# Second products of five groups of a fused FNet and SwiGLU block put into Strassen's form

## The chip, the cores and the metric

The kernel runs on one core of a Trainium2 chip. The metric is device time in microseconds of one execution, taken over several runs. The core's engines are named as in the profile: PE (TensorE, matmuls), PEld (its weight loads), DVE (VectorE), ACT (ScalarE), POOL (GpSimd) and SP (SyncE, which here issues loads). Each works off its own queue of instructions in order.

## The reference

One block of a network on 2048 rows of 512 columns, in float32. The condition `c` gives six vectors, shifts, scales and gates. The first half is a Fourier mixing of the modulated layer norm, the second a gated feed-forward with 1792 inner columns:

```python
x = x + ga * _A_ref(h, ...)                   # real part of a DFT over rows and columns
h = _layernorm(x, axis=-1) * (1 + cb) + sb
gate = jnp.einsum("bsd,df->bsf", h, w1)       # "first products"
up   = jnp.einsum("bsd,df->bsf", h, w3)
hh   = _silu(gate) * up
out  = jnp.einsum("bsf,fd->bsd", hh, w2)      # "second products"
x = x + gb * out
```

The change touches only the feed-forward, and in it only the second products.

## The kernel before

**Precision.** A float32 operand is split into a high part (an ACT copy that rounds to fp32r, `copy`, L87) and a low part (a DVE subtraction, `minus`, L90). `product` (L98, its matmul in L100) then makes three passes: high by high, high by low, low by high. The weights are the stationary operand, the activations move.

**Tiles.** Everything is held with columns on the 128 partitions and rows along the free dimension, in row blocks t = 0 to 3 of 512 rows. The inner 1792 columns are seven groups g of 256. Row blocks are worked in two pairs, (0, 2) as pair 0 and (1, 3) as pair 1. An item is a group with a pair. Items 0 to 4 are groups 2 to 6 of pair 0, items 5 to 11 are groups 0 to 6 of pair 1.

**First products of an item.** They are already in the Strassen-Winograd form: seven units a1 to a7 for w1 and b1 to b7 for w3, made by `factor`. A unit is six matmuls into one PSUM bank (two column blocks of 128 by three passes). The units chain: a6, a7 and a4 are added in the bank of a1 after the running sum was read, a3 in that of a5. The left operands are w, and sums of quarters of w (`w1s`, `w3s`), each with its high and low; the right operands are the normalized rows h2 and sums of them (h2h, h2l, th, tl). The units' banks are copied or added out by ACT (x, L87; Silu into v, L1224) and DVE (x and v, L93; v<-v,x, L96). `result` makes the product v of gate and up and then its parts hf, the high on ACT and the low on DVE.

**Second products before.** For each row block t and each block d of 128 output columns there is one unit, `down_unit`: six matmuls (two inner column blocks by three passes) into one bank, banks 6 and 7 in turn. So there are eight units, called y in the order, to an item. ACT copies the bank, scaled by gb, into half of a tile y (L335), and after every second unit POOL issues an accumulating DMA (L1146) of the 512 KB tile y into a buffer `sums` in HBM. Each row block and half of the output columns has such a buffer. The last two groups of pair 1 don't go to HBM: their units are added by DVE (L1137) to a tile xr, which `load_sums` (L1106) fetches from `sums` after group 4.

**What sets the order.** The units are written out by hand, one string to an item (`body`, after a `head` that ends the item before):

```python
body = "a6 a5 y a7 y y a4 y a3 y b1 y b2 y b6 b5 y"          # L1661
head = ... else "-b7 a1 a2 -b4 -b3 " if i else "a1 a2 "       # L1666
```

A minus means a unit of the item before. The y units in a body belong to the item before too, so the second products of items 5 to 9 stand in the bodies of items 6 to 10. Below, "the first to the fifth body" are these, each counted from its first unit, -b7, to the next body's. Item 5, where the pair changes, is `turning`.

Preparing a weight is five steps (`weight_jobs`, L1164): the high (ACT), four sums of quarters (DVE, 128x256 each), the low (DVE), the high of the sums (ACT), the low of the sums (DVE). w2 had two (`plain_jobs`): high and low. Steps wait in a list `jobs`. After each unit `beside` lets as many of them out as a credit of DVE and ACT time allows (`advance`), and where a unit needs a weight that isn't ready, `drain` lets everything ahead of it out at once. w1 of the next item is put in the list at a3, w2 of the same item at b2, w3 of the next item at b3. `behind(n, fn)` issues an operation n units later.

## Time and profile before

The time is 708.48 us, the median of 3 runs (707.67 to 708.64). The profiled execution took 708.46 us; its span, from the first to the last instruction, is 706.7 us, so 1.8 us lie around it.

| stretch, us | what runs | PE busy | DVE busy | ACT busy | DMA share |
|---|---|---|---|---|---|
| 60 to 276 | DFT over rows | 214.18 of 216.00 | 191.66 | 123.39 | 0.63 |
| 276 to 477 | feed-forward, mostly pair 0 | 197.15 of 201.00 | 166.60 | 134.40 | 0.56 |
| 477.00 to 501.25 | item 5, where the pair changes | 24.25 of 24.25 | 15.79 | 17.73 | 0.78 |
| 501.25 to 652.63 | the first to the fifth body | 151.17 of 151.38 | 92.34 | 92.36 | 0.59 |
| 652.63 to 706.70 | the last group and the end | 45.91 of 54.07 | 31.18 | 13.71 | 0.29 |

How to read it: a matmul of 512 columns is shown 0.39 us long, but the next starts 0.227 us after it, so busy times of PE overlap and a stall under 0.16 us does not show as idle time. The distance from start to start is the measure. On DVE and ACT, too, the next instruction can start shortly before the shown end of the one ahead. The DMA share is the mean busy share of the 16 DMA engines.

### The profile page before, as it was taken

What the parts mean: (1) busy time and instruction counts of PE and PEld (TensorE: products, weight loads), DVE (VectorE), ACT (ScalarE), POOL (GpSimd) and SP (SyncE); (2) the same over time, 40 slices, a digit from 0 to 9 for tenths busy, and PEclk for the clock granted to TensorE, in tenths of its full rate; (3) what the DMA queues carried; (4) which work ended last, traced back from release to release, by engine and by line L of the source; (5) the groups of instructions that cost most, each with busy time, mean ns of one, the idle gap of its engine ahead of it and who ended that gap; (6) DMA issues with size and microseconds to landing.
All of it is one profiled execution on the core that took longest, in us unless ns stands there. A gap on an engine that the chain in (4) does not pass through costs nothing.

```text
span 706.7 us, 8912 instructions
## 1 busy us (share of the span) xinstructions
PE 686.3 (97%) x3152; PEld 564.7 (80%) x3152; DVE 548.3 (78%) x877; ACT 430.8 (61%) x709; POOL 119.4 (17%) x141
## 2 busy tenths in 40 slices
PE   7999999999999999899999999999999999999995
PEld 4898888888888888687888788787788888888784
DVE  5999679997999978579987886896865556664763
ACT  4998865545454655745677676867665565656420
POOL 1320253542524000200100101011010100101000
PEclk9999999999999999999999999999999999999998
DMA  8730299796678521522868558376763847537403
GB/s 266 211 120 1 77 373 328 251 307 229 207 283 287 168 86 41 92 58 64 209 114 199 89 130 153 61 156 137 239 136 73 180 62 175 111 69 162 137 0 124
DMA packets 38100, 108.93 MB, mean 154 GB/s; under 512 B 4896, under 2 KB 5152, under 8 KB 38048
## 3 DMA queue, kind: packets, MB, share of 16 engines
q0 software_dynamic: 12352, 43.00, 29.3%
q1 hardware_dynamic: 25264, 63.98, 27.5%
q10 hardware_dynamic: 432, 1.31, 0.5%
q8 instruction: 26, 0.43, 0.3%
q14 instruction: 26, 0.21, 0.1%
HBM read 76.81 MB, written 33.55 MB: 156 GB/s over the span
## 4 chain that ended last, share of the span: by engine, by line
PE 81%; DVE 7%; ACT 6%; issue 2%; DMA 2%; SPq 1%; ACTq 0%; DVEq 0%
PE bank L100 52%; PE bank L750 25%; PE bank L559 2%; PE bank L598 1%; DMA wmr<-in_wmr 1%; ACT xc L894 1%; PE bank L576 1%; DVE xc L96 1%; SPq L231 1%; ACT hf L87 1%; ACT y L335 1%; DVE v L96 0%; DVE hl L90 0%; ACT hm L501 0%; DMA w<-in_wdi 0%
## 5 line engine op out<-in xcount | busy, mean ns | idle before, releaser
L100 PE MATMUL bank<-hf,w2h 128*128 128x512 f32 (+1 forms) x452 | 140.9, 391 | 0.3
L1146 POOL DMA_DIRECT2D sum<-y x48 | 41.0, 855 | 390.1 <-ACT y L335 373.0
L100 PEld LDWEIGHTS bank<-hf,w2h 128*128 128x128 f32 x452 | 84.3, 188 | 22.1 <-DVE hf L90 3.4
L100 PE MATMUL bank<-hf,w2l 128*128 128x512 f32 (+1 forms) x226 | 87.6, 388 | 0.0
L87 ACT ACTIVATE hf<-v 128x512 fp32r<-128x512 f32 x56 | 35.3, 630 | 67.3 <-DVE v L96 62.7
L335 ACT ACTIVATE y<-bank,gb 128x512 f32<-128x512 f32 x96 | 64.9, 682 | 18.6 <-PE bank L100 18.3
L93 DVE TENSOR_TENSOR v<-bank,x 128x512 f32<-128x512 f32 x36 | 24.7, 685 | 34.9 <-PE bank L100 34.8
L750 PE MATMUL bank<-bh,us 128*128 128x512 f32 x128 | 49.9, 390 | 0.0
L93 DVE TENSOR_TENSOR x<-bank,x 128x512 f32<-128x512 f32 x36 | 24.7, 687 | 32.4 <-PE bank L100 28.7
L750 PE MATMUL bank<-bh,ul 128*128 128x512 f32 x128 | 49.8, 389 | 0.0
L750 PE MATMUL bank<-d,us 128*128 128x512 f32 x128 | 49.8, 389 | 0.0
L750 PE MATMUL bank<-d,uh 128*128 128x512 f32 x128 | 49.8, 389 | 0.0
L750 PE MATMUL bank<-l,us 128*128 128x512 f32 x128 | 49.8, 389 | 0.0
L750 PE MATMUL bank<-l,uh 128*128 128x512 f32 x128 | 49.8, 389 | 0.0
L100 PEld LDWEIGHTS bank<-hf,w2l 128*128 128x128 f32 x226 | 42.4, 188 | 8.4
L90 DVE TENSOR_TENSOR hf<-v,hf 128x512 fp32r<-128x512 f32 x56 | 38.5, 687 | 12.2 <-ACT hf L87 12.1
L170 POOL DMA_INDIRECT re<-in_ctr,mirror x32 | 35.8, 1117 | 66.2 <-DVE ul L90 39.5
L1224 ACT ACTIVATE v<-v 128x512 f32<-128x512 f32 x36 | 22.8, 632 | 38.8 <-DVE v L93 38.8
L87 ACT ACTIVATE x<-bank 128x512 f32<-128x512 f32 x72 | 41.4, 586 | 7.2 <-PE bank L100 6.5
L170 POOL DMA_INDIRECT im<-in_cti,mirror x32 | 32.7, 1023 | 35.3 <-PE bank L750 10.0
L100 PE MATMUL bank<-h2h,w1h 128*128 128x512 f32 x80 | 31.8, 397 | 1.5 <-ACT h2h L87 1.5
L100 PE MATMUL bank<-h2l,w1h 128*128 128x512 f32 x80 | 31.9, 399 | 0.8 <-DVE h2l L90 0.8
(246 smaller groups left out, 1775.2 us busy)
## 6 DMA issues: line engine op xcount, KB each, us to landing
sum<-y POOLq DMA_DIRECT2D x48, 512.0 KB, 5.6
w<-in_w SPq DMA_DIRECT2D x42, 512.0 KB, 4.5
re<-in_ctr SPq DMA_DIRECT2D x32, 256.0 KB, 5.0
im<-in_cti SPq DMA_DIRECT2D x32, 256.0 KB, 5.0
wmc<-in_wmc SPq DMA_DIRECT2D x8, 512.0 KB, 6.3
xr<-in_xt SPq DMA_DIRECT2D x8, 512.0 KB, 7.6
sum<-xr SPq DMA_DIRECT2D x8, 512.0 KB, 6.2
x<-in_x SPq DMA_DIRECT2D x11, 256.0 KB, 4.8
```

Source lines behind the costliest of these rows:

```text
L87: nc.scalar.activation(dst, src, AF.Copy, scale=scale)
L90: nc.vector.tensor_tensor(out=dst, in0=a, in1=b, op=OP.subtract)
L93: nc.vector.tensor_tensor(out=dst, in0=a, in1=b, op=OP.add)
L96: nc.vector.tensor_tensor(out=dst, in0=a, in1=b, op=OP.mult)
L100: nc.tensor.matmul(acc, lhs[a], rhs[b], start=first and n == 0, stop=last and n == len(PASSES) - 1, skip_group_check=more,)
L170: nc.gpsimd.indirect_dma_start(dst, None, rows, bass.IndirectOffsetOnAxis(ap=at, axis=0))
L231: queue.dma_start(raw_w[dt][q * 64 : (q + 1) * 64, m, :], w[i][par::2, q])
L335: nc.scalar.activation(dst, src, AF.Identity, scale=by)
L559: nc.tensor.matmul(halves(hb[k])[:, m, :], sides((hh, hl)[a][k])[:, dt, m, :], wu[dt][:, b, m, :], start=False, stop=dt % 2 == 1 and n == ...
L750: nc.tensor.matmul(acc[what, e], lhs, rhs, start=begin and i == 0, stop=(end or (turn and what == "x")) and i == len(terms) - 1, skip_grou ...
L1146: nc.gpsimd.dma_start(sums[t, d // 2], y, accum_op=OP.add)
L1224: behind(k != 0 or q == 0, lambda: nc.scalar.activation(v, src, AF.Silu))
```

## The change

The second products of items 5 to 9 (groups 0 to 4 of pair 1, `SEVEN`) take the same form as the first ones: seven units (`seven_unit`) in place of eight, in the order 2, 5, 3, 1, 6, 7, 4. A unit is again six matmuls: two output column blocks e, in banks 6 and 7, by three passes. Units 2, 5 and 1 start the two banks anew. The others are added to what stands there after it was read: 3 to 5, and 6, 7 and 4 to 1. ACT reads both banks after every unit, so there are 14 copies to a group in place of 8 and 7 accumulating DMAs in place of 4.

The right operands are three of the products v as they are and four sums of them, made by DVE in place in the tiles v (`seven_parts`, spread over eight units); each of the seven gets a high and a low, before there were four. The left operands are w2 and sums of its quarters, so w2 takes the five steps of `seven_jobs` in place of two. In the turning item w2 is put in the list at b3 in place of b2. In items 6 to 9 w3 of the next item is put there at b6, at the end of the body, in place of b3. The bodies with seven y have the order `"a6 a5 a7 y a4 y a3 y b1 y b2 y b6 y b5 y"`. `load_sums` for both row blocks comes after the last unit.

```diff
--- before.py
+++ after.py
@@ -1208,6 +1208,12 @@
     TO = {1: 0, 6: 0, 7: 0, 4: 0, 2: 1, 5: 2, 3: 2}
     state, vs = {}, {}
 
+    SEVEN = [(g, 1) for g in range(NG - 2)]
+    ORDER7 = (2, 5, 3, 1, 6, 7, 4)
+    LEFT7 = {1: "h0", 2: "h2", 4: "h3", 5: "s0", 6: "s1", 7: "s2", 3: "s3"}
+    TO7 = {2: (0, 0), 5: (1, 1), 3: (0, 1), 1: (0, 0), 6: (0, 1), 7: (1, 1), 4: (1, 0)}
+    right7, banks7 = {}, []
+
     def right(pair, n):
         t0, t1 = PAIRS[pair]
         if n in (1, 2, 3):
@@ -1224,6 +1230,9 @@
             behind(k != 0 or q == 0, lambda: nc.scalar.activation(v, src, AF.Silu))
             return
         times(v, v, src)
+        if (g, pair) in SEVEN:
+            seven_parts(i, q, k)
+            return
 
         def highs():
             hf[g, PAIRS[pair][k], q] = take(F32R, "hf")
@@ -1235,6 +1244,105 @@
 
         behind(1, highs)
         behind(2, lows)
+
+    def seven_parts(i, q, k):
+        key = items[i]
+        v = {(a, b): vs[i][a][:, b, :] for a in range(2) for b in range(2)}
+
+        def high(n, src):
+            right7[key, n] = take(F32R, "hf")
+            copy(right7[key, n][:, 0, :], src)
+
+        def low(n, src):
+            u = right7[key, n]
+            minus(u[:, 1, :], src, u[:, 0, :].bitcast(F32))
+
+        if (q, k) != (0, 1):
+            n = {(0, 0): 1, (1, 0): 2, (1, 1): 3}[q, k]
+            behind(1, lambda: high(n, v[q, k]))
+            behind(2, lambda: low(n, v[q, k]))
+            return
+        t1, t2, t3, t4 = v[0, 0], v[1, 1], v[0, 1], v[1, 0]
+        behind(1, lambda: minus(t1, v[0, 1], v[0, 0]))
+        behind(2, lambda: high(5, t1))
+        behind(2, lambda: minus(t3, v[1, 1], v[0, 1]))
+        behind(3, lambda: low(5, t1))
+        behind(3, lambda: minus(t2, v[1, 1], t1))
+        behind(4, lambda: high(7, t3))
+        behind(4, lambda: minus(t4, v[1, 0], t2))
+        behind(5, lambda: high(6, t2))
+        behind(5, lambda: low(7, t3))
+        behind(6, lambda: high(4, t4))
+        behind(7, lambda: low(6, t2))
+        behind(8, lambda: low(4, t4))
+
+    def seven_jobs(key):
+        use = wuse[key] = {}
+
+        def highs():
+            use["h"] = take(F32R, "w2h")
+            copy(flat(use["h"]), flat(wraw[key]))
+
+        def totals():
+            use["s"] = take(F32, "w2s")
+            s, r = four(use["s"]), four(wraw[key])
+            plus(s[:, 0, :], r[:, 1, :], r[:, 3, :])
+            minus(s[:, 1, :], s[:, 0, :], r[:, 0, :])
+            minus(s[:, 2, :], r[:, 0, :], r[:, 1, :])
+            minus(s[:, 3, :], r[:, 2, :], s[:, 1, :])
+
+        def lows():
+            use["l"] = take(F32R, "w2l")
+            r = wraw.pop(key)
+            minus(flat(use["l"]), flat(r), flat(use["h"]).bitcast(F32))
+            give(r)
+
+        def sum_highs():
+            use["sh"] = take(F32R, "w2sh")
+            copy(flat(use["sh"]), flat(use["s"]))
+
+        def sum_lows():
+            use["sl"] = take(F32R, "w2sl")
+            minus(flat(use["sl"]), flat(use["s"]), flat(use["sh"]).bitcast(F32))
+            give(use.pop("s"))
+            done.add((key, "l"))
+
+        step(jobs, 1, highs, 0.0, 1.0)
+        step(jobs, 1, totals, 1.4)
+        step(jobs, 1, lows, 1.2)
+        step(jobs, 1, sum_highs, 0.0, 1.0)
+        step(jobs, 1, sum_lows, 1.2)
+
+    def seven_unit(g, pair, n, key):
+        new = n in (1, 2, 5)
+        if new:
+            banks7[:] = [bank(6), bank(7)]
+        y = take(F32, "y")
+        which, k = TO7[n]
+        t = PAIRS[pair][k]
+        names = ("h", "l") if LEFT7[n][0] == "h" else ("sh", "sl")
+        u = right7.pop(((g, pair), n))
+        for e, to in enumerate(banks7):
+            at = int(LEFT7[n][1]) * HALF + e * P
+            product(
+                to,
+                [flat(wuse[key][x])[:, at : at + P] for x in names],
+                [u[:, b, :] for b in range(2)],
+                new,
+                True,
+                not new,
+            )
+            d = 2 * which + e
+            copy_by(y[:, e, :], to, gb[:, d : d + 1])
+        give(u)
+        nc.gpsimd.dma_start(sums[t, which], y, accum_op=OP.add)
+        behind(4, lambda: give(y))
+        if n == ORDER7[-1]:
+            for x in wuse.pop(key).values():
+                give(x)
+            if g == NG - 3:
+                for t in PAIRS[pair]:
+                    load_sums(t)
 
     def factor(i, w, n):
         g, pair = items[i]
@@ -1280,7 +1388,7 @@
             behind(1, lambda: give(st["x"]))
             if w == "w3":
                 for x in vs.pop(i):
-                    behind(3, lambda x=x: give(x))
+                    behind(9 if items[i] in SEVEN else 3, lambda x=x: give(x))
 
 
     loads.extend((n, m) for n in range(len(steps)) for m in range(2))
@@ -1576,10 +1684,14 @@
                 up_block(g, t, q, w)
                 beside(2.72, USED[w])
 
-    def down(g, pair, t, d, key):
+    def down(g, pair, *which):
+        key = which[-1]
         drain(lambda: (key, "l") in done, jobs)
         delayed()
-        down_unit(g, pair, t, d, key)
+        if (g, pair) in SEVEN:
+            seven_unit(g, pair, *which)
+        else:
+            down_unit(g, pair, *which)
         beside(1.36, USED["own" if pair == 1 and g >= NG - 2 else "y"])
 
     for w in ("w1", "w3"):
@@ -1617,6 +1729,9 @@
             for n in PLACE:
                 give(h.pop((0, n)))
         sum_parts(jobs, *sums_of.pop())
+
+    def early_w3(i):
+        return items[i] in SEVEN and i != turning
 
     def unit(kind, i, n):
         g, pair = items[i]
@@ -1638,8 +1753,8 @@
         if (kind, n) == ("a", 3) and more:
             load_w(("w3", *items[i + 1]))
             weight_jobs(i + 1, "w1")
-        if (kind, n) == ("b", 2):
-            plain_jobs(("w2", g, pair))
+        if (kind, n) == ("b", 3 if i == turning else 2):
+            (seven_jobs if (g, pair) in SEVEN else plain_jobs)(("w2", g, pair))
         if (kind, n) == ("b", 3):
             if i + 2 == turning:
                 drain(lambda: ("xc", 3) in done)
@@ -1648,10 +1763,15 @@
                 sums_of.append(pair_sums(background, 1))
             if i + 1 == turning:
                 other_operands()
-            if more:
+            if more and not early_w3(i):
                 weight_jobs(i + 1, "w3")
-            for t in PAIRS[pair]:
-                seconds.extend((g, pair, t, d, ("w2", g, pair)) for d in range(ND))
+            if (g, pair) in SEVEN:
+                seconds.extend((g, pair, n, ("w2", g, pair)) for n in ORDER7)
+            else:
+                for t in PAIRS[pair]:
+                    seconds.extend((g, pair, t, d, ("w2", g, pair)) for d in range(ND))
+        if (kind, n) == ("b", 6) and more and early_w3(i):
+            weight_jobs(i + 1, "w3")
         beside(1.36, FACTOR[kind][n])
 
     weight_jobs(0, "w3")
@@ -1659,6 +1779,8 @@
     ln2(3)
     for i in range(len(items)):
         body = "a6 a5 y a7 y y a4 y a3 y b1 y b2 y b6 b5 y"
+        if i and items[i - 1] in SEVEN:
+            body = "a6 a5 a7 y a4 y a3 y b1 y b2 y b6 y b5 y"
         if i == turning:
             body = "y y y y y a6 y a5 y a7 y b1 b2 a4 b6 a3 b5"
         if i == len(items) - 1:
```

How the queues change is shown at two places. The first is DVE's queue in the first body. The rows stand between the product v of b3 and the addition that reads a7's bank (`v_...<-bank0`); w3s, w3l and w3sl are the sums and the lows of w3 for this body, w2s, w2l and w2sl those of w2, hf the lows of the products. Before:

```order
L93 TENSOR_TENSOR w3s_717_4617<-w3_700_4539 128x256
L90 TENSOR_TENSOR w3s_717_4617<-w3s_717_4617,w3_700_4539 128x256
L90 TENSOR_TENSOR w3s_717_4617<-w3_700_4539 128x256
L90 TENSOR_TENSOR w3s_717_4617<-w3_700_4539,w3s_717_4617 128x256
L90 TENSOR_TENSOR hf_715_4605<-v_661_4328,hf_715_4605 128x512
L90 TENSOR_TENSOR w3l_720_4634<-w3_700_4539,w3h_716_4615 128x1024
L90 TENSOR_TENSOR hf_718_4623<-v_660_4327,hf_718_4623 128x512
L90 TENSOR_TENSOR w3sl_724_4648<-w3s_717_4617,w3sh_721_4636 128x1024
L93 TENSOR_TENSOR v_712_4584<-bank0_709_4575,x_723_4646 128x512
```

The same stretch with the change; `v_660<-v_660`, `v_660<-v_661,v_660` and `v_661<-v_661,v_660` are the first three sums of products:

```order
L93 TENSOR_TENSOR w2s_715_4613<-w2_687_4444 128x256
L90 TENSOR_TENSOR w2s_715_4613<-w2s_715_4613,w2_687_4444 128x256
L90 TENSOR_TENSOR w2s_715_4613<-w2_687_4444 128x256
L90 TENSOR_TENSOR w2s_715_4613<-w2_687_4444,w2s_715_4613 128x256
L90 TENSOR_TENSOR hf_713_4601<-v_661_4328,hf_713_4601 128x512
L90 TENSOR_TENSOR v_660_4327<-v_660_4327 128x512
L90 TENSOR_TENSOR w2l_717_4629<-w2_687_4444,w2h_714_4611 128x1024
L90 TENSOR_TENSOR v_660_4327<-v_661_4328,v_660_4327 128x512
L90 TENSOR_TENSOR w2sl_722_4645<-w2s_715_4613,w2sh_718_4631 128x1024
L90 TENSOR_TENSOR hf_719_4633<-v_660_4327,hf_719_4633 128x512
L90 TENSOR_TENSOR v_661_4328<-v_661_4328,v_660_4327 128x512
L93 TENSOR_TENSOR v_710_4580<-bank0_707_4571,x_721_4643 128x512
```

Where w3's preparation stood, w2's stands with three sums and a low between its steps, and the addition from a7's bank follows all of it; w3's preparation comes behind.

The second place is ACT's queue at the end of the second to fourth body, from the high of b2's product (hf) on. x are copies of the banks of b6 and b5, y copies of the second products' banks. Before, from the second body:

```order
L87 ACTIVATE hf_788_5000<-v_754_4819 128x512
L335 ACTIVATE y_789_5002<-bank6_790_5003,gb_152 128x512
L87 ACTIVATE x_782_4974<-bank3_781_4967 128x512
L87 ACTIVATE x_792_5026<-bank5_791_5019 128x512
L335 ACTIVATE y_789_5002<-bank7_793_5028,gb_152 128x512
```

And with the change, in the second body; y_803, y_808 and y_814 are the tiles of units 6, 7 and 4:

```order
L87 ACTIVATE hf_802_5043<-v_769_4867 128x512
L335 ACTIVATE y_803_5045<-bank6_796_5015,gb_152 128x512
L335 ACTIVATE y_803_5045<-bank7_797_5016,gb_152 128x512
L87 ACTIVATE w2sh_805_5057<-w2s_801_5038 128x1024
L87 ACTIVATE x_794_5011<-bank3_793_5004 128x512
L87 ACTIVATE w3h_807_5069<-w3_787_4979 128x1024
L335 ACTIVATE y_808_5071<-bank6_796_5015,gb_152 128x512
L335 ACTIVATE y_808_5071<-bank7_797_5016,gb_152 128x512
L87 ACTIVATE x_811_5093<-bank5_810_5086 128x512
L87 ACTIVATE w3sh_813_5097<-w3s_809_5081 128x1024
L335 ACTIVATE y_814_5099<-bank6_796_5015,gb_152 128x512
```

Five instructions have become eleven, and two preparing steps stand between the copies of unit 6 and those of unit 7, a third between those of 7 and 4.

## Prediction, on record before the run

> **What bounds the kernel now.** I read the share of the engines first, then the windows of the five bodies, then single rows of the timeline.
>
> ```profile
> span 706.7 us, 8912 instructions
> PE 686.3 (97%) x3152; PEld 564.7 (80%) x3152; DVE 548.3 (78%) x877; ACT 430.8 (61%) x709; POOL 119.4 (17%) x141
> ```
>
> Then the windows of the five bodies, a row each: length, then busy time of PE, PEld, DVE, ACT, POOL, the granted clock, the DMA share and GB/s.
>
> ```profile
> 501.25:531.97 30.72, 30.51 (x134) 24.62 (x132) 20.94 (x32) 19.40 (x29) 2.56 (x3) 1.00 0.63 162
> 531.97:562.13 30.16, 30.16 (x133) 24.70 (x132) 17.85 (x27) 18.25 (x27) 3.40 (x4) 1.00 0.59 122
> 562.13:592.30 30.17, 30.17 (x133) 24.70 (x132) 17.85 (x27) 18.24 (x27) 3.41 (x4) 1.00 0.59 122
> ...
> 622.46:652.63 30.17, 30.17 (x133) 24.70 (x132) 17.85 (x27) 18.23 (x27) 3.41 (x4) 1.00 0.52 99
> ```
>
> PE is never without work there, and DVE and ACT have 12 us free of 30. So PE's own time is what a body costs. How much is that to a unit?
>
> ```profile
> 503.44 0.50 PE L100 MATMUL bank<-h2h,w1l 128*128 128x512 f32 x1 [0.21 <-DVE w1l L90]
> ...
> 508.60 0.39 PE L100 MATMUL bank<-th,w1sh 128*128 128x512 f32 x1
> ...
> 509.96 0.39 PE L100 MATMUL bank<-th,w1sh 128*128 128x512 f32 x1
> ...
> 602.84 0.19 PEld L100 LDWEIGHTS bank<-hf,w2h 128*128 128x128 f32 x1 [0.38 <-DVE hf L90]
> ```
>
> The rows at 508.60 and 509.96 are the first matmuls of a6 and a5: a unit takes 1.36 us, a matmul 0.227. A body of 22 units would be 29.92 us. The 0.25 to 30.17 is one wait for the low of a product (last row); the first body has 0.55 more at a1, which waits for w1's low (first row).
>
> **What the change removes.** Five units, 30 matmuls: 6.80 us, if nothing else waits. A body of 21 units is 28.56 us.
>
> **What it adds.** To each group, on ACT, 6 copies y, 3 highs and one high of w2's sums; on DVE 3 lows, 4 sums of products, 4 sums of quarters and one low. The prices are distances from start to start, where instructions stand back to back:
>
> ```profile
> 508.80 0.69 DVE L93 TENSOR_TENSOR x<-bank,x 128x512 f32<-128x512 f32 x1 [0.67 <-PE bank L100]
> 509.52 0.69 DVE L96 TENSOR_TENSOR v<-v,x 128x512 f32<-128x512 f32 x1
> 510.13 0.42 DVE L93 TENSOR_TENSOR w3s<-w 128x256 f32<-128x256 f32 x1
> 510.59 0.43 DVE L90 TENSOR_TENSOR w3s<-w3s,w 128x256 f32<-128x256 f32 x1
> 510.93 0.42 DVE L90 TENSOR_TENSOR w3s<-w 128x256 f32<-128x256 f32 x1
> 511.27 0.42 DVE L90 TENSOR_TENSOR w3s<-w,w3s 128x256 f32<-128x256 f32 x1
> 511.60 0.68 DVE L90 TENSOR_TENSOR hf<-v,hf 128x512 fp32r<-128x512 f32 x1
> 512.21 1.22 DVE L90 TENSOR_TENSOR w3l<-w,w3h 128x1024 fp32r<-128x1024 f32 x1
> 513.34 0.68 DVE L90 TENSOR_TENSOR hf<-v,hf 128x512 fp32r<-128x512 f32 x1
> 513.94 1.22 DVE L90 TENSOR_TENSOR w3sl<-w3s,w3sh 128x1024 fp32r<-128x1024 f32 x1
> ```
>
> On DVE: 0.61 for 128x512 (0.72 where the next needs its result), 1.47 for four sums of quarters, 1.13 for 128x1024.
>
> ```profile
> 602.28 1.06 ACT L87 ACTIVATE w3sh<-w3s 128x1024 fp32r<-128x1024 f32 x1 [0.41 <-DVE w3s L90]
> 603.24 0.58 ACT L87 ACTIVATE x<-bank 128x512 f32<-128x512 f32 x1
> 603.72 0.68 ACT L335 ACTIVATE y<-bank,gb 128x512 f32<-128x512 f32 x1
> ...
> 610.43 0.69 ACT L335 ACTIVATE y<-bank,gb 128x512 f32<-128x512 f32 x1 [0.76 <-PE bank L100]
> 611.01 1.05 ACT L87 ACTIVATE w1h<-w 128x1024 fp32r<-128x1024 f32 x1
> ...
> 618.81 0.64 ACT L87 ACTIVATE hf<-v 128x512 fp32r<-128x512 f32 x1 [1.30 <-DVE v L96]
> 619.35 0.67 ACT L335 ACTIVATE y<-bank,gb 128x512 f32<-128x512 f32 x1
> ```
>
> On ACT: 0.96 for a high of a weight, 0.48 for x, 0.58 for y, 0.54 for hf. No row shows the sums of products as such; the lows (687 ns mean) and v<-v,x (692) have the same shape, which bounds them within 1%. So a group's ACT work grows by 6 x 0.58 + 3 x 0.54 + 0.96 = 6.1 us and DVE's by 7 x 0.61 + 1.47 + 1.13 = 6.9. On the busy rows that is 24.3 and 24.8 of 28.56 us: enough in sum, but with little left for a bad place. What counts, then, is where work is in front of something that PE waits for. A hand-over costs this:
>
> ```profile
> 323.49 0.57 ACT L87 ACTIVATE x<-bank 128x512 f32<-128x512 f32 x1
> ...
> 324.11 0.19 PEld L100 LDWEIGHTS bank<-th,w1sh 128*128 128x128 f32 x1 [0.65 <-ACT x L87]
> ...
> 324.45 0.40 PE L100 MATMUL bank<-tl,w1sh 128*128 128x512 f32 x1
> ...
> 592.30 0.39 PE L100 MATMUL bank<-th,w3sh 128*128 128x512 f32 x1
> ...
> 592.50 0.69 ACT L335 ACTIVATE y<-bank,gb 128x512 f32<-128x512 f32 x1 [0.76 <-PE bank L100]
> ```
>
> The copy ends at 324.06 and the second matmul after it is at 324.45, so the first began in effect at 324.22: 0.16 us after the end. In the other direction a reader starts 0.20 us after the next unit's first matmul.
>
> **First body, DVE.** Up to v<-v,x at 509.52 nothing has changed. Behind it the order now has four sums of w2, a low, a sum, w2's low, a sum, the low of w2's sums, a low, a sum, and only then the addition that reads a7's bank. From 510.13: +1.47 is 511.60, +0.61 +0.61 is 512.82, where w2's low starts; it ends at 514.04. The first y unit is three units after 508.60 and its third matmul, the first with that low, 0.45 later, at 513.13; it starts at 514.20, 1.07 late. DVE goes on: 512.82 + 1.13 + 0.60 + 1.14 + 0.61 + 0.61 = 516.91 for the addition, which ends at 517.60. Unit a4 is added in the bank that it reads, so a4 starts at 517.76, where the order alone would give 508.60 + 4 x 1.36 = 514.04: **3.72 us late**, the 1.07 included. Before, this was covered: w3 was not needed before b1, and two y units stood between a7 and a4.
>
> Behind it ACT is late too. After the addition it has a Silu and two copies of unit 2 (517.63 + 0.54 + 2 x 0.58 = 519.33), then the high of w3's sums (0.96; they are ready at 519.1), a high (0.54), a Silu out of a bank (0.48, as x) and a high (0.54), and only at 521.85 the first copy of unit 5, which lets PE in at 521.85 + 0.68 + 0.16 = 522.69. Unit 3, which is added in that bank, was due at 517.76 + 3 x 1.36 = 521.84: **0.85 late**. The preparation of w3, now behind, costs nothing: its low ends at 520.8 and b1 starts at 524.1.
>
> **End of the first four bodies, ACT.** Let E be the end of b2. DVE adds at E + 0.20, multiplies at + 0.72, and hf starts after another 0.72, at E + 1.64. Then hf 0.54, two copies of unit 6 (1.16), w2sh 0.96, x 0.48, w3h 0.96: the first copy of unit 7 starts at E + 5.74, ends at E + 6.42 and lets unit 4 in at E + 6.58. Unit 7 was due at E + 2.72 and gets its bank at E + 1.64 + 0.54 + 0.67 + 0.16 = E + 3.01. Unit 4 was due at E + 5.44. So PE loses 0.29 and then 0.85, **1.14 us a body**.
>
> The Trainium skill, Perfetto Trace Analysis, section "Matmuls", says that independent matmul groups should rotate through different PSUM banks, so that copying one out overlaps the next. The chain does the opposite, seven units in the same two banks, and by that rule the 0.85 of the first body and the 1.14 of four are its price; with more banks the forecast would be 5.4 us lower.
>
> **Second to fifth body, DVE.** b3 ends 6.80 us into the body. Then come the addition at 7.00, the product at 7.72, a low at 8.33, a sum at 8.94, a sum that overwrites an operand of that one and so waits for its end (9.66), a low that waits for ACT's high of the first sum (9.66 + 0.63, so 10.33), a sum at 10.94 and the addition of a7's bank, 11.55 to 12.24. With the hand-over a4 starts at 12.40, due 9 x 1.36 = 12.24: 0.16 late.
>
> **The sum.** First body: 30.72 + 3.72 + 0.85 + 1.14 - 1.36 = 35.07, less the 0.25 of the wait that its order no longer has, **34.82: +4.10**. Second to fourth: 28.56 + 0.16 + 1.14 = 29.86, **-0.31 each**. Fifth: the next group's w2 takes two steps and w3 comes later, so only the 0.16 and 0.29 remain: 29.01, **-1.16**. Together 4.10 - 0.93 - 1.16 = **+2.0 us**, on the profiled 708.46, which agrees with the median 708.48: **710.5 us**.
>
> **What I cost at nothing.** DMA:
>
> ```profile
> q0 software_dynamic: 1729, 6.29, 44.4%
> q1 hardware_dynamic: 1296, 4.72, 14.8%
> ...
> sum<-y POOLq DMA_DIRECT2D x12, 512.0 KB, 5.6
> w<-in_w SPq DMA_DIRECT2D x9, 512.0 KB, 4.5
> ```
>
> These are three bodies (531.97 to 622.46, 90.5 us): an accumulating DMA takes 0.444 x 90.5 / 12 = 3.35 us of all 16 engines, a load 1.49. Seven and three are 27.9 us of a body of 29.9. They hide as long as the tiles come free in time. By the same working of the two queues the tile of unit 5 is filled 16.8 us into a body and next written (by w3sh) at 29.4, that of unit 3 at 19.4 and 30.5, so a landing may take 11 us against the 5.6 in the row. The sums into one buffer wait for each other on POOL (unit 6 for unit 3, two y units apart); that is 5.4 us against 5.6 and delays only POOL's queue, whose issues are 7 x 0.85 us. If the cover fails, each us is a us of ACT or DVE. The loads of xr come behind the last unit together; the second is used 15 us into the last group, after a landing of 5.6 and a load of 4.5: nothing, or up to 1 us. SP's other loads stand where they stood.
>
> **The rivals.**
>
> 1. *Not slower: ACT keeps ahead at the end of the bodies.* Its place is the stretch from hf after b2 to unit 4, which I put together from pairs seen apart. If the banks come free by E + 5.28 in place of E + 6.42, the 1.14 goes in four bodies, 4.6 us: 705.9 us. For it speaks that ACT had 12 us free; against it that the queue is fixed and six instructions would have to be done in 3.6 us that take 4.8. 12%.
> 2. *The sums saturate the DMA engines.* 27.9 us of 29.9 leave no margin. If transfers get 15% longer beside each other (32.1 us), a body is DMA-bound, 2.2 us over my 29.86 in four: 719 us. Against it: the cover of 11 us, and that the busy share counts a packet's time, not the rate it could have. 12%.
> 3. *PE's clock drops.* The first row of bodies shows two waits of PE at a granted clock of 1.00. If several waits to a body brought it to 0.9 (a number chosen for the price), a body's 28.56 us would be 31.7, 3.2 more in each of five: 726 us. 3%.
>
>    The Trainium skill, TensorE: Matmul & The Clock Gate, section "A second HAM failure mode: psum-queue depth-cycling", describes this for a kernel that idles shortly between matmul groups on changing banks. The waits in the trace did not bring it on.
> 4. *The saving is not there.* PE's order has 30 matmuls fewer, so this is out.
>
> **The chances.** 73% for the forecast, with a range of its own of 708.4 to 712.4: the first body's wait hangs on a chain of twelve instructions (0.5 us either way), a body's end on eight (0.3 us, four times). 0.2% is 1.4 us and about what a measurement of this kernel can tell from no change. The forecast's case gives 0.02 faster, 0.22 same, 0.49 slower; rival 1 gives 0.10 faster and 0.02 same; 2 and 3 are slower. Faster 0.12, same 0.24, slower 0.64. The range from 705.9, rival 1, to 713.0 leaves out rivals 2 and 3 and a few per cent of the forecast.
>
> **What would show it.** In the first body a wait of PE for DVE v (the addition) of 2 us or more before a4, one of about 1 us for w2l, and ACT y ahead of unit 3; in the second to fourth body a wait for ACT y of about 0.8 us before the last y unit; a fifth body near 29 us; body lengths 34.8, 29.9 three times, 29.0. Wrong would be the sum if the first body is under 32 us (DVE's chain doesn't hold PE), if the middle bodies are at 28.6 (rival 1), or over 31 with POOL or ACT waiting for DMA (rival 2).

## The result, and the profile after

The changed kernel took 711.60 us, the median of 6 runs (709.24 to 713.50), against 707.52 for the kernel before in the same series: a ratio of 1.0057 (95% interval 1.0042 to 1.0071). It is slower, by about 4 us. The forecast was 710.5 us, slower.

The profiled execution took 709.24 us. The page's first lines, with span and shares:

```profile
span 707.4 us, 9004 instructions
PE 680.8 (96%) x3122; PEld 556.5 (79%) x3122; DVE 582.8 (82%) x937; ACT 456.4 (65%) x759; POOL 132.7 (19%) x156
```

PE does 30 matmuls fewer and is busy 5.5 us less, DVE 34.5 us more and ACT 25.6 more, and the span is 0.7 us longer. The windows of the five bodies of this kernel, with the columns as in the prediction:

```profile
499.49:534.32 34.83, 30.40 (x128) 23.18 (x127) 33.20 (x55) 27.31 (x42) 4.94 (x6) 1.00 0.65 143
534.32:564.28 29.96, 29.35 (x127) 23.41 (x126) 24.78 (x40) 23.28 (x38) 5.95 (x8) 1.00 0.81 174
564.28:594.25 29.97, 29.36 (x127) 23.42 (x126) 24.79 (x40) 23.29 (x38) 5.96 (x8) 1.00 0.85 173
594.25:624.22 29.97, 29.36 (x128) 23.42 (x127) 24.79 (x40) 23.29 (x38) 5.96 (x8) 1.00 0.85 182
624.22:653.38 29.16, 29.06 (x128) 23.49 (x126) 20.26 (x30) 21.70 (x36) 6.14 (x8) 1.00 0.83 173
```

The sum is 153.89 us where it was 151.38: **+2.51**. The first body alone is 4.11 longer, and DVE, 20.94 us busy in it before, is busy 33.20. The next three give 0.2 each, the fifth 1.0. Where PE waits in the first body (rows of its timeline that show idle time):

```profile
501.67 0.50 PE L100 MATMUL bank<-h2h,w1l 128*128 128x512 f32 x1 [0.21 <-DVE w1l L90]
512.28 0.50 PE L100 MATMUL bank<-hf,w2l 128*128 128x512 f32 x1 [0.79 <-DVE w2l L90]
515.83 0.50 PE L100 MATMUL bank<-th,w1h 128*128 128x512 f32 x1 [2.33 <-DVE v L93]
520.70 0.73 PE L100 MATMUL bank<-hf,w2sh 128*128 128x512 f32 x2 [0.49 <-ACT y L335]
532.82 0.73 PE L100 MATMUL bank<-hf,w2h 128*128 128x512 f32 x2 [0.51 <-ACT y L335]
```

The first row is a1's wait, as before the change; the others are those of the first y unit, a4, unit 3 and unit 4 of the prediction. The idle time shown is short by the overlap of shown durations, so I take distances of starts beyond 0.227 us a matmul, with the 0.12 that is lost again behind each wait: 1.06 for w2l, 2.60 for a4, 0.78 for unit 3, 0.38 for unit 7 (which shows no idle time), 0.78 for unit 4.

What stands in front of a4 on DVE: the four sums of w2's quarters start at 508.34, w2's low at 511.01, and then, up to the addition from a7's bank,

```profile
512.75 1.22 DVE L90 TENSOR_TENSOR w2sl<-w2s,w2sh 128x1024 fp32r<-128x1024 f32 x1
513.88 0.69 DVE L90 TENSOR_TENSOR hf<-v,hf 128x512 fp32r<-128x512 f32 x1
514.48 0.69 DVE L90 TENSOR_TENSOR v<-v,v 128x512 f32<-128x512 f32 x1
515.09 0.69 DVE L93 TENSOR_TENSOR v<-bank,x 128x512 f32<-128x512 f32 x1
```

with no idle time between any two of them.

The end of the second body, in ACT's timeline. b2's product ends on DVE shortly before 557.99; y at 558.52 are unit 6's two copies, at 562.05 unit 7's:

```profile
557.99 0.63 ACT L87 ACTIVATE hf<-v 128x512 fp32r<-128x512 f32 x1 [0.76 <-DVE v L96]
558.52 1.25 ACT L335 ACTIVATE y<-bank,gb 128x512 f32<-128x512 f32 x2
559.66 1.06 ACT L87 ACTIVATE w2sh<-w2s 128x1024 fp32r<-128x1024 f32 x1
560.62 0.59 ACT L87 ACTIVATE x<-bank 128x512 f32<-128x512 f32 x1
561.09 1.07 ACT L87 ACTIVATE w3h<-w 128x1024 fp32r<-128x1024 f32 x1
562.05 1.27 ACT L335 ACTIVATE y<-bank,gb 128x512 f32<-128x512 f32 x2
```

From hf to unit 7's first copy are 4.06 us, where the prediction had put 4.10 together from pairs. PE's rows at the same place:

```profile
558.76 0.39 PE L100 MATMUL bank<-th,w3sl 128*128 128x512 f32 x1
559.25 0.74 PE L100 MATMUL bank<-hf,w2sh 128*128 128x512 f32 x2
...
561.89 0.39 PE L100 MATMUL bank<-th,w3sl 128*128 128x512 f32 x1
562.79 0.73 PE L100 MATMUL bank<-hf,w2h 128*128 128x512 f32 x2 [0.51 <-ACT y L335]
```

Unit 7 starts 0.49 after the matmul ahead of it, unit 4 0.90, where 0.227 would do.

DMA in the second to fourth body, the shares and the landing:

```profile
q0 software_dynamic: 3033, 11.05, 68.3%
...
sum<-y POOLq DMA_DIRECT2D x22, 512.0 KB, 5.7
```

The sums land as fast as before (5.7 us, 5.6 then) though there are 22 of them in place of 12. The loads of w take longer, 6.9 us in place of 4.5.

**Why the profile shows +0.7 and the medians +4.1.** In the profile of before two stretches ran at half clock; the same places of the profile after did not. Windows of before, then of after:

```profile
72.22:75.63 3.41, 3.41 (x18) 3.41 (x17) 2.84 (x4) 2.29 (x5) 0.00 (x0) 0.50 0.00 0
...
297.50:300.92 3.42, 2.95 (x7) 2.37 (x8) 2.74 (x7) 1.96 (x2) 1.03 (x2) 0.50 1.11 177
```

```profile
70.59:74.00 3.41, 2.17 (x17) 2.14 (x18) 3.41 (x6) 2.93 (x6) 0.00 (x0) 1.00 0.00 0
...
295.87:299.29 3.42, 2.38 (x9) 1.55 (x10) 2.73 (x3) 3.04 (x4) 1.03 (x2) 1.00 1.05 193
```

So the first body begins 1.76 us earlier after the change, at 499.49 and not 501.25, by nothing that the change did. The profiles' +0.7 is the bodies' +2.5 less this 1.76. The medians rise by 4.1, 1.6 more than the bodies, and the profiled execution of the change is the shortest of its six. The runs below look for the rest.

### The profile page after: what moved, and what is told of

It is laid out like the page before. It is cut to its first block, busy times and chain, and to the rows that moved or that the text cites. A ratio compares the mean times of both kernels' runs of the same rounds, so it can differ in the third digit from the quotient of the medians.

```text
span 707.4 us, 9004 instructions
## 1 busy us (share of the span) xinstructions
PE 680.8 (96%) x3122; PEld 556.5 (79%) x3122; DVE 582.8 (82%) x937; ACT 456.4 (65%) x759; POOL 132.7 (19%) x156
## 4 chain that ended last, share of the span: by engine, by line
PE 75%; DVE 10%; ACT 9%; issue 3%; DMA 2%; SPq 1%; DVEq 0%; ACTq 0%
PE bank L100 47%; PE bank L750 25%; ACT y L335 2%; PE bank L559 1%; PE bank L598 1%; DMA w<-in_wdr 1%; ACT xc L894 1%; ACT hf L87 1%; DVE v L96 1%; DVE x L93 1%; ACT w3h L87 1%; DVE xc L96 1%; ACT x L87 1%; SPq L231 1%; DMA x<-in_x 1%
## 5 line engine op out<-in xcount | busy, mean ns | idle before, releaser
L100 PE MATMUL bank<-hf,w2h 128*128 128x512 f32 (+1 forms) x352 | 109.4, 391 | 2.3 <-ACT y L335 2.0
L335 ACT ACTIVATE y<-bank,gb 128x512 f32<-128x512 f32 x126 | 82.3, 690 | 8.1 <-PE bank L100 7.8
L87 ACT ACTIVATE hf<-v 128x512 fp32r<-128x512 f32 x71 | 44.7, 630 | 62.8 <-DVE v L96 57.2
L100 PEld LDWEIGHTS bank<-hf,w2h 128*128 128x128 f32 x352 | 65.2, 188 | 19.9 <-ACT y L335 4.7
L1146 POOL DMA_DIRECT2D sum<-y x28 | 24.0, 857 | 246.4 <-ACT y L335 233.5
L100 PE MATMUL bank<-hf,w2l 128*128 128x512 f32 (+1 forms) x176 | 68.3, 388 | 0.8 <-DVE w2l L90 0.8
L90 DVE TENSOR_TENSOR hf<-v,hf 128x512 fp32r<-128x512 f32 x71 | 48.9, 688 | 17.6 <-ACT hf L87 17.5
L1338 POOL DMA_DIRECT2D sum<-y x35 | 29.8, 852 | 132.2 <-ACT y L335 124.3
L170 POOL DMA_INDIRECT im<-in_cti,mirror x32 | 33.5, 1046 | 35.4 <-PE bank L750 9.9
L100 PEld LDWEIGHTS bank<-hf,w2l 128*128 128x128 f32 x176 | 33.1, 188 | 7.8 <-DVE w2l L90 1.2
```

The lines of the kernel that those rows point to most:

```text
L87: nc.scalar.activation(dst, src, AF.Copy, scale=scale)
L90: nc.vector.tensor_tensor(out=dst, in0=a, in1=b, op=OP.subtract)
L100: nc.tensor.matmul(acc, lhs[a], rhs[b], start=first and n == 0, stop=last and n == len(PASSES) - 1, skip_group_check=more,)
L170: nc.gpsimd.indirect_dma_start(dst, None, rows, bass.IndirectOffsetOnAxis(ap=at, axis=0))
L335: nc.scalar.activation(dst, src, AF.Identity, scale=by)
L1146: nc.gpsimd.dma_start(sums[t, d // 2], y, accum_op=OP.add)
```

## The experiments

Each ratio is to runs of the kernel before on the same chip. Body lengths are from each kernel's profile; a star marks a body in which the clock was halved for a while. The medians belong to several series, in which the kernel before took 707.5 to 710.5 us, so only the ratios can be compared.

| kernel | five bodies, us | sum | median, us | ratio (95%) |
|---|---|---|---|---|
| before | 30.72, 30.16, 30.17, 30.17, 30.16 | 151.38 | 707.52 | 1 |
| the change | 34.83, 29.96, 29.97, 29.97, 29.16 | 153.89 | 711.60 | 1.0057 (1.0042 to 1.0071) |
| again | 34.82, 29.96, 29.96, 29.96, 29.15 | 153.85 | 711.37 | 1.0052 (1.0034 to 1.0070) |
| group0_plain | 30.77, 30.31, 29.93, 29.96, 29.14 | 150.11 | 706.15 | 0.9979 (0.9964 to 0.9993) |
| w3_at_b3 | 34.01, 35.43*, 34.29*, 34.30*, 34.26* | 172.29 | 730.05 | 1.0308 (1.0282 to 1.0335) |
| w2_at_b2 | 37.27*, 29.99, 29.94, 29.97, 29.16 | 156.33 | 717.35 | 1.0102 (1.0084 to 1.0120) |
| w3_at_b5 | 35.71*, 29.76, 29.74, 29.76, 29.76 | 154.73 | 711.87 | 1.0037 (1.0020 to 1.0054) |
| hf_late | 36.96*, 30.26, 30.30, 30.27, 29.16 | 156.95 | 713.93 | 1.0051 (1.0031 to 1.0071) |
| four_sums_out | 34.84, 29.98, 29.93, 29.94, 29.12 | 153.81 | 711.05 | 1.0050 (1.0032 to 1.0068) |
| wait_alone | 34.90*, 30.16, 30.17, 30.17, 30.16 | 155.56 | 711.95 | 1.0066 (1.0045 to 1.0086) |
| both | 30.79, 29.55, 29.80, 29.79, 29.74 | 149.67 | 706.11 | 0.9974 (0.9956 to 0.9993) |
| spread | 31.15, 29.76, 29.77, 30.60, 29.14 | 150.42 | 707.86 | 0.9996 (0.9984 to 1.0009) |
| group0_plain_2 | 30.83, 29.75, 29.98, 29.95, 29.79 | 150.30 | 709.95 | 0.9986 (0.9974 to 0.9998) |
| spread_2 | 30.65, 29.95, 29.95, 29.95, 29.78 | 150.28 | 709.50 | 0.9984 (0.9972 to 0.9995) |

The theory, as on record: what the change costs is the place of preparing work on DVE and ACT, in front of operations that PE waits for. The rivals: the new form itself costs it (two chained banks, more DMA), or the clock.

### The first body: is it DVE's order?

**group0_plain** keeps the first of the five groups as it was.

```diff
-    SEVEN = [(g, 1) for g in range(NG - 2)]
+    SEVEN = [(g, 1) for g in range(1, NG - 2)]
```

> Group 0 of pair 1 keeps the eight plain units, the other four groups stay in Strassen's form. Theory place (the first body pays for w2's five steps and three sums in front of one addition): the first body falls from 34.81 to 30.7 to 31.3 us, the other four stay at 29.98, 29.97, 29.97 and 29.16; 3.5 to 4.1 us less than the changed kernel. Rival, the cost is that of the form (two chained banks, seven accumulating DMAs) in every group alike: the change loses a fifth of its cost, 0.5 us, and the first body stays over 33.

Measured: 30.77 us in the first body, 30.31 in the second (a4 waits 0.36 longer there than in the change, which I had not foreseen), the others unchanged; the sum of the bodies is 3.78 below the change, and the time is below that of before. The cost was the first group's alone, four groups in the new form give time back. On this chip the median is 5.2 us below that of the changed kernel ("again", below), more than the 3.7 that the bodies give; the mean granted clock is 0.9932 here and 0.9915 there.

**w3_at_b3** leaves out the one edit that keeps w3's steps away from the sums of products.

```diff
     def early_w3(i):
-        return items[i] in SEVEN and i != turning
+        return False
```

> The changed kernel with w3 of the next item put in the list at b3 everywhere, as before the change. Theory place: in the second to fifth body w3's steps now stand in front of the addition that reads a7's bank, 1.47 + 1.13 + 1.14 = 3.7 us of DVE, so that a4 comes 3.9 us late there, as in the first body; ahead of unit 3 ACT's y may hold PE for a further 0.8, and the 0.8 ahead of unit 4 goes: 32.9 to 33.8 us in the second to fourth body, 32.9 in the fifth, 34.0 in the first; 11 to 14 us more than the changed kernel. Rival, the first body's wait is the start of the new form itself (its first group has empty banks and tiles) and not DVE's order: the bodies stay within 0.5 us of 30 and 29.2.

Measured: 34.01 in the first body, as expected, and 34.3 to 35.4 in the others. DVE's queue in the second body, from b3's product to the addition of a7's bank (550.58), and the wait of PE for it:

```profile
543.23 0.69 DVE L96 TENSOR_TENSOR v<-v,x 128x512 f32<-128x512 f32 x1
543.84 0.42 DVE L93 TENSOR_TENSOR w3s<-w 128x256 f32<-128x256 f32 x1
...
546.51 1.22 DVE L90 TENSOR_TENSOR w3l<-w,w3h 128x1024 fp32r<-128x1024 f32 x1
547.64 0.69 DVE L90 TENSOR_TENSOR v<-v,v 128x512 f32<-128x512 f32 x1
548.25 1.22 DVE L90 TENSOR_TENSOR w3sl<-w3s,w3sh 128x1024 fp32r<-128x1024 f32 x1
...
550.58 0.69 DVE L93 TENSOR_TENSOR v<-bank,x 128x512 f32<-128x512 f32 x1
```

```profile
551.33 0.80 PE L100 MATMUL bank<-th,w1h 128*128 128x512 f32 x1 [3.42 <-DVE v L93]
```

By starts the wait is 3.58 us, and every body behind the first gets what only the first had. DVE has no more to do for it: in the third body it is busy 24.64 us, in the change 24.79, and the body takes 34.29 us in place of 29.97. That decides for DVE's order, against "the first group of a new form" and against the sum of DVE's work. The bodies are 0.5 to 1.6 us over the range that I gave, since each has a stretch at half clock behind that wait (last part); a single stretch takes 1.6 us, and without it they would be at 32.7.

**w2_at_b2** takes back the other edit of the order.

```diff
-        if (kind, n) == ("b", 3 if i == turning else 2):
+        if (kind, n) == ("b", 2):
```

> The changed kernel with w2 of the turning item put in the list at b2, as before the change. Theory place: w2's steps now come in front of w1's on DVE, and w3's take w2's place in front of the addition from a7's bank, a chain of the same length: the first body's wait ahead of a4 stays at 2.5 to 3.7 us, w2l's wait of 1.06 ahead of the first y goes into it, and 1 to 2 us come on at a1 for w1's low: 34.8 to 36.8 us, the other bodies as they are. Rival, it was the move of w2 to b3 that made the first body long: with w2 at b2 the first body is 32 us or less.

PE's waits of 1 us or more:

```profile
507.29 0.50 PE L100 MATMUL bank<-h2h,w1l 128*128 128x512 f32 x1 [1.87 <-DVE w1l L90]
523.04 0.50 PE L100 MATMUL bank<-th,w1h 128*128 128x512 f32 x1 [3.42 <-DVE v L93]
```

Measured: 37.27, with a stretch at half clock behind the first wait; without its 1.6 us that is 35.7, inside what the theory gave. The wait ahead of a4 stays, now with w3's steps in front of it, and a1 waits as well. So the move to b3 was worth its place; it chose which of two weights jams a4.

### The end of the bodies: is it ACT's queue?

**w3_at_b5** puts w3's preparation behind unit 7's copies.

```diff
-        if (kind, n) == ("b", 6) and more and early_w3(i):
+        if (kind, n) == ("b", 5) and more and early_w3(i):
```

> w3 of the next item is put in the list at b5 in place of b6, so that its two highs on ACT come behind the copies of units 7 and 4 and not in front of them. Theory place: the wait of 0.8 us ahead of unit 4 goes in the first four bodies: 34.0, then three times 29.15, the fifth stays at 29.16; 3.3 us less than the changed kernel, as long as w3's lows are then still ready for the next b1. Rival, the two chained banks themselves make PE wait (two copies in a row after each unit): the bodies stay within 0.2 us of 29.97. Second rival, w3 is now late for a use: a wait for w3's low appears in place of the other.

Measured: 29.76 in place of 29.97, not 29.15. The wait ahead of unit 4 is gone; its 0.78 has given 0.2. A new one stands at the next body's unit -b4, seen in PE's row at the start of the second body and in DVE's at the same place of the fourth:

```profile
541.58 0.50 PE L100 MATMUL bank<-th,w3h 128*128 128x512 f32 x1 [0.22 <-DVE x L93]
```

```profile
599.20 1.23 DVE L90 TENSOR_TENSOR w3sl<-w3s,w3sh 128x1024 fp32r<-128x1024 f32 x1 [0.87 <-ACT w3sh L87]
600.34 0.68 DVE L93 TENSOR_TENSOR x<-bank,x 128x512 f32<-128x512 f32 x1
```

DVE, in order, stands 0.87 us waiting for ACT's high of w3's sums, and the addition that reads -b7's bank, in which -b4 is added, is queued behind. It costs 0.48 by starts, and a4 is later too. The fifth body, which had no wait to lose, gets 0.6 longer by it. So the place was rightly named, and the second rival came nearest: the wait moved on, though it is not w3 that is late for its use but the addition behind w3's low.

**hf_late** asks whether units 7 and 4 wait for two things or for one queue.

```diff
-            behind(1, lambda: high(n, v[q, k]))
-            behind(2, lambda: low(n, v[q, k]))
+            late = n == 1
+            behind(1 + late, lambda: high(n, v[q, k]))
+            behind(2 + late, lambda: low(n, v[q, k]))
```

> The changed kernel with the high of b2's product one unit later, behind unit 6's two copies on ACT in place of in front of them. Theory queue (what unit 4 waits for is the sum of ACT's work between b2 and unit 7's copies, whatever its order): unit 7's wait of 0.38 us goes, but unit 4's grows by as much in the first four bodies, which keep 34.8 and 30.0; only the fifth, where unit 4 doesn't wait, gets 0.3 to 0.4 shorter (28.8). In all 0.4 us less than the changed kernel. Rival, the two waits are apart: 0.4 us in each of five bodies, 1.9 in all.

PE at the end of the second body:

```profile
566.91 0.73 PE L100 MATMUL bank<-hf,w2h 128*128 128x512 f32 x2 [1.23 <-ACT y L335]
```

Unit 7's wait is gone, unit 4's has grown from 0.78 to 1.50 by starts; the body is 0.3 longer. Of the growth 0.38 is what unit 7 had, as the theory said. The rest comes of a wait on ACT that the change doesn't have there: w2sh now comes up before DVE has made w2's sums.

```profile
563.27 1.07 ACT L87 ACTIVATE w2sh<-w2s 128x1024 fp32r<-128x1024 f32 x1 [0.94 <-DVE w2s L90]
```

So it is one queue, but not the sum of its work "whatever its order": hf had filled the time until w2's sums were ready. The fifth body is unchanged, where I expected 0.4 less: b2 there belongs to item 10, whose group is not in the new form, and the edit doesn't reach it.

### Is it DMA?

**four_sums_out** issues four of seven sums; the output lacks the other three products.

```diff
-        nc.gpsimd.dma_start(sums[t, which], y, accum_op=OP.add)
+        if n in (2, 3, 1, 4):
+            nc.gpsimd.dma_start(sums[t, which], y, accum_op=OP.add)
```

> The changed kernel with the accumulating DMAs of units 5, 6 and 7 left out (three of seven to a group), so that those products don't reach the output; all else is issued. Theory place: DMA is hidden, the bodies stay at 34.8, 30.0 three times and 29.2 within 0.1 us, and the time within 0.5 us. Rival, the sums of DMA hold ACT or DVE: the bodies shrink, by up to 1.4 us each.

The third body, and the queue in the second to fourth:

```profile
567.59:597.52 29.93, 29.31 (x127) 23.42 (x126) 24.78 (x40) 23.25 (x38) 3.41 (x4) 1.00 0.57 122
```

```profile
q0 software_dynamic: 1728, 6.29, 41.3%
```

Measured: the queue's share falls from 68.3% to 41.3%, no body changes by more than 0.04 us, and the ratio of 1.0050 is that of the change. DMA is hidden in these bodies, at a share of 0.81 to 0.85 where the prediction's 27.9 us of 29.9 would be 0.93. The rival of the saturated engines falls.

### Is it the clock?

**again** is the changed kernel a second time, with no edit.

> The changed kernel a second time, for the spread of its runs (709.2 to 713.5 us). Theory clock: the five bodies repeat within 0.1 us in the profile (34.8, 30.0 three times, 29.2), and each run's span times its granted clock stays within 702.5 to 704, so that the spread is short stretches at half clock, about 1.7 us apiece. Rival: the spread is waits of engines or DMA; then span times clock is spread as wide as the times, over 3 us, and a profiled run of another time has another body length.

The bodies repeat within 0.01 us. But this profiled execution, too, is the shortest of its six, so it doesn't show the bodies of a longer one. The six runs spread from 709.16 to 713.32, and span times clock from 702.4 to 705.1, wider than the theory had it and narrower than the times, so these products decide nothing. The mean clock of the six is 0.9915, that of the 26 runs of the kernel before beside them 0.9925.

**wait_alone** makes one wait of PE in the kernel before, and nothing else.

```diff
-            minus(flat(use["sl"]), flat(use["s"]), flat(use["sh"]).bitcast(F32))
+            for _ in range(4 if (w, i) == ("w3", 6) else 1):
+                minus(flat(use["sl"]), flat(use["s"]), flat(use["sh"]).bitcast(F32))
```

> The kernel before the change, with one thing added: the low of w3's sums for the first body is computed four times in place of once, 3 x 1.14 us of DVE in front of the addition from a7's bank. PE waits once for 2.4 to 2.7 us before a4, and nothing else differs. Theory clock, a wait of this length sets off a stretch at half clock in part of the executions: the mean granted clock falls by about 0.002 (0.9925 to 0.9905) and the median rises by 1 to 2 us more than the wait, 3.5 to 4.5 us in all. Rival, the lower clock of the changed kernel comes of something else (more work on ACT, DVE and DMA): the clock stays at 0.992 to 0.993 and the median rises by 2.4 to 2.7 us.

PE behind the wait, and then two windows around it (the seventh value is the granted clock):

```profile
518.82 0.80 PE L100 MATMUL bank<-th,w1h 128*128 128x512 f32 x1 [2.42 <-DVE v L93]
```

```profile
515.15:518.57 3.42, 1.25 (x6) 0.71 (x4) 3.35 (x4) 0.00 (x0) 0.00 (x0) 1.00 0.00 0
518.57:521.98 3.41, 3.16 (x8) 2.50 (x9) 0.19 (x1) 1.98 (x4) 0.86 (x1) 0.50 0.23 19
```

Measured: matmuls 0.43 us apart for 3.41 us, a first body 4.18 longer of which 2.58 are the wait, a median 4.17 us above that of before, and a mean clock of 0.9922 against 0.9940. One wait of 2.6 us costs 4.2. The theory holds, and its size too: in the profile the dip of the clock takes 1.6 us.

### A version that beats both

**both** joins group0_plain and w3_at_b5, with the two diffs shown.

> Group 0 plain and w3 at b5, both edits together. Theory place: the two gains add: bodies of 30.7 to 31.3, three times 29.15 and 29.16; 6.8 to 7.4 us less than the changed kernel, 3 to 5 us less than before the change. Rival, the sums of DMA or of ACT's work bound a body at 29.9: the second gain doesn't come, 3.5 to 4 us less than the changed kernel.

Measured: a ratio of 0.9974 (0.9956 to 0.9993); the bodies give 1.7 us, 0.24%. The gains add, but the second is small: the five bodies are 0.44 us shorter than those of group0_plain alone, and in time the two kernels can't be told apart (0.9974 and 0.9979). I gave 3 to 5 us less than before the change; it is 2.2.

**spread** keeps all five groups in the new form and moves the preparations.

```diff
-        if (kind, n) == ("b", 3 if i == turning else 2):
+        if (kind, n) == ("b", 1 if i == turning else 2):
...
-            if more and not early_w3(i):
+            if more and not early_w3(i) and i != turning:
...
-        if (kind, n) == ("b", 6) and more and early_w3(i):
+        if (kind, n, i) == ("a", 7, turning + 1):
+            weight_jobs(i, "w3")
+        if (kind, n) == ("b", 5 if i < 9 else 6) and more and early_w3(i):
```

> All five groups in the new form, with the preparations spread otherwise: w2 of the turning item at b1, w3 of item 6 at its own a7, w3 of items 7 to 9 at b5, of item 10 at b6. Theory place: in the first body only sums and lows of products stand in front of the addition from a7's bank, so a4's wait falls from 3.7 to 0.2 us; w1's low comes 0.3 later; w3's two highs on ACT keep the 0.8 ahead of unit 3 or cost as much at b1: 30.0 to 31.0 us; then 29.75 three times and 29.15: 4.5 to 5.5 us less than the changed kernel's profile, and with no long wait the clock of before: 704.5 to 706. Rival, DVE's and ACT's sums of work and not places limit the first body: 33 us or more there, and 707 to 709 in all.

PE's waits in the first body, and there is none ahead of a4:

```profile
505.01 0.50 PE L100 MATMUL bank<-h2h,w1l 128*128 128x512 f32 x1 [0.89 <-DVE w1l L90]
520.48 0.74 PE L100 MATMUL bank<-hf,w2sh 128*128 128x512 f32 x2 [0.49 <-ACT y L335]
```

Measured: 31.15 in the first body, with the wait ahead of a4 gone. By itself this run doesn't part place from the sum of work: w2's steps have gone to item 5, so DVE is busy 29.49 us in this body and no longer 33.20, 3.7 less, and the body is 3.7 shorter; in both it is idle for 1.6 to 1.7 us only. w3_at_b3 parts them. The length is a little over what I gave, since w1's low comes 0.7 us later still and not 0.3. The fourth body is 30.60, because the step at b6 in item 9 falls into this body, where I had counted it in the next. In time it equals the kernel before (707.86 against 707.78 on that chip), where I gave 704.5 to 706.

**group0_plain_2** and **spread_2** add hf_late's edit to "both" and to "spread", and do the high of w3's sums ahead of w3's low; spread_2 also has w2 of the turning item at a7 and w3 of every later item at b5.

```diff
+        if w == "w3" and early_w3(i - 1):
+            step(jobs, 1, sum_highs, 0.0, 1.0)
+            step(jobs, 1, lows, 1.2)
...
-        if (kind, n) == ("b", 3 if i == turning else 2):
+        if (kind, n) == (("a", 7) if i == turning else ("b", 2)):
```

> Group 0 plain, w3 at b5 with the high of its sums in front of its low, and the high of b2's product one unit later. Theory place: bodies of 30.8, 29.2, and three of 29.4 (29.76 less unit 7's 0.38); 148.2 us for the five, 3.2 less than before the change, and no wait over 1 us, so that the clock is that of before. Rival: unit 7's wait turns into another, and the bodies stay at 29.55 and 29.75.

> All five groups in the new form; w2 of the turning item at its a7, so that its steps are done before w1's; w3 of item 6 at its own a7; the other w3 at b5 with the high of its sums in front of its low; the high of b2's product one unit later. Theory place: first body 29.8 to 30.3 (31.15 of the earlier spread kernel less 0.7 of a1's wait and 0.38 of unit 7's), then four times 29.4: 147.3 to 147.9 us for the five, 3.5 to 4 less than before the change. Rival: w2 is now in front of something that item 5 waits for, and the 0.7 comes back there.

Measured: bodies of 29.75 to 29.98, not 29.4 or less. Unit 7's wait went to unit 4 once more (0.56 there), and ACT waits 0.94 for w2's sums, as in hf_late, which ran beside them. The wait at -b4 stays too (0.52), so the new order of w3's two steps took nothing from it. spread_2's first body is 30.65, over the 29.8 to 30.3 that I gave; its wait for w1's low is back at 0.48, as in the change, so w2 at a7 is early enough, and what is over is unit 4's 0.55. The two beat the kernel before by 0.14 and 0.16%; the intervals overlap that of "both", so the three can't be ranked.

## Why the prediction was right, and where it was off

- **First body.** Predicted 34.82, measured 34.83. Terms: w2l 1.07 (1.06), a4 3.72 with that (3.66), unit 3 0.85 (0.78), the end 1.14 (0.38 + 0.78 = 1.16). group0_plain shows by taking away, and w3_at_b3 by adding with DVE's work unchanged, that it is DVE's chain in front of one addition.
- **Second to fourth body.** Predicted 29.86, measured 29.97. The end was 1.16 there too, split otherwise than on record (0.29 + 0.85). Unit 7's wait and unit 4's are one queue (hf_late), so the split matters little. The 0.11 over stands behind the waits, where some twenty matmuls start 229 to 236 ns after the one ahead and not 227.
- **Fifth body.** Predicted 29.01, measured 29.16.
- **The sum of the bodies.** Predicted +2.0, measured +2.51; the 0.5 is three times 0.11 and once 0.15.
- **DMA at nothing.** Right: four_sums_out.
- **The two banks.** The Trainium skill, Perfetto Trace Analysis, section "Matmuls", with its rule that independent matmul groups should rotate through banks, had been given all of the waits for ACT's y as their price. w3_at_b5 takes unit 4's wait away with the same two banks; unit 7's 0.38 stays. For unit 4 it is the preparing work in front of the copies that costs; more banks were not tried.
- **The step that failed: "The waits in the trace did not bring it on."** The rival of the clock was priced at a lasting 0.9 (726 us) and set aside at 3%, since the waits of before, 0.55 us at most in these bodies, had not lowered it there. The same profile has the clock at 0.50 at 72 and 297 us, outside the bodies, and the prediction doesn't reckon with that. The change makes waits of 1.06 and 2.60 us close together, and wait_alone shows what a wait of that size can do: one stretch of 3.41 us at half clock, 1.6 us. The two profiled executions of the change had none in their bodies; w3_at_b5 and hf_late, whose first body has the same two waits, had. Over the 2.5 us of the bodies the medians leave 1.6 us in the first series (4.1) and 0.5 in the second (3.0). That this remainder is such stretches fits wait_alone, the mean clocks and group0_plain, but no profile of the change shows it. The twelve runs of w3_at_b5 fall in two heaps, four from 707.89 to 709.32 and eight from 710.96 to 712.87; their means lie 3.6 us apart, more than one stretch, and what parts them isn't shown.
- **The time.** The forecast of 710.5 is 1.1 us under the measured 711.60. But the change was put at +2.0 and came out at +4.1, and the base of 708.48, a median of three runs, lies 0.96 above the 707.52 of the six. That hides nearly half of the miss, and it is luck.
- **The base.** The sum was made on one profiled execution. It had two half-clock stretches of its own (72 and 297 us), and the profile after had neither: a difference of 1.76 us between two profiles that no edit made.

## What to carry to other kernels

Before an engine with time to spare is given more work, list what will stand in its queue in front of each operation that PE waits for: here 59 us of free time on each of DVE and ACT, of 151, didn't help where the steps of w2 and three sums of products stood in front of one addition, and moving work out of one gap mostly moved the wait to the next in-order queue (w3_at_b5, hf_late). A saving of whole matmuls is worth its units less the waits: 1.36 us a group came out as 1.0 at best (the fifth body of the change) and as 0.2 in its middle three (0.4 to 0.6 in "both"), and the first group lost 4.1. And a long wait of PE can cost more than its length (2.6 us cost 4.2 in wait_alone), so compare several executions, body by body, before a difference of under 0.5% is put down to the edit.

## What the hardware showed

The half-clock stretches follow a rule that all fourteen profiles of the table keep. Their starts lie on a grid of 3.413 us that runs through an execution and begins at another point in each. I cut 60 to 695 us of each profile on its own grid and summed the matmuls' time at full clock, 0.227 us each, in every window. In 27 windows the sum was 1.33 us or less, and behind each of them the clock was 0.50 for the next window; in the others, over 2500, it was 1.34 or more, and behind none was it. Both values hang on how a matmul is counted and can shift by some hundredths. The second window of a double stretch fits as well, if a matmul at half clock counts 0.227 there too. The limit is about 39% of a window in these profiles. Two windows of w3_at_b5, at the first body's waits:

```profile
512.89:516.31 3.42, 1.73 (x7) 0.77 (x5) 3.42 (x5) 2.59 (x5) 0.00 (x0) 1.00 0.00 0
516.31:519.72 3.41, 1.98 (x5) 1.60 (x6) 3.38 (x9) 2.00 (x4) 0.00 (x0) 0.50 0.00 0
```

and two of the change, where the grid lay otherwise over the same waits:

```profile
510.91:514.32 3.41, 1.80 (x7) 0.84 (x5) 3.41 (x5) 2.66 (x5) 0.00 (x0) 1.00 0.00 0
514.32:517.73 3.41, 1.90 (x8) 1.61 (x9) 3.38 (x8) 1.92 (x4) 0.00 (x0) 1.00 0.00 0
```

By the starts, the first window of w3_at_b5 has 1.26 us of work and the first of the change 1.34. (The busy time shown, 1.73 and 1.80, counts each matmul at 0.39 and can't tell them apart.) For the two waits of the first body, 0.94 and 2.50 us with 1.05 between them, 2.7 of the 3.4 us of possible positions give a window with 2.08 us or more of idle time: an estimate of four executions in five, if each position is as likely as another. The profiles don't bear that out. Of the six with these two waits (the change, again, four_sums_out, w3_at_b3, w3_at_b5 and hf_late) two had a stretch there, and in all fourteen a point of the grid lies 0.93 to 1.49 us behind the start of the first body. So the positions there are not spread evenly, and how often the change meets the stretch stays open.

The Trainium skill, TensorE: Matmul & The Clock Gate, section "What's actually happening", has the window of 3413 ns and that it runs free; the traces agree. The section "HAM oscillation — how this bites in real kernels" gives the rule as no PE-idle gaps over about 3.4 us. Here the measurement differs: 2.1 to 2.8 us of waiting in one window were enough.
